# A two-layer attention and MLP kernel with its order written by a planner: four key passes, a second query block opened early, softmax sums by DMA, halved last blocks

## The chip, the cores and the metric

One core of a Trainium2 chip. The metric is the device time of one execution in microseconds; the shown time is the median of several runs. PE is the matrix engine (TensorE), ACT the scalar engine, DVE the vector engine, POOL GpSimd, SP the engine that issues most DMAs.

## The reference

Batch 1, 2048 rows, 448 columns, 16 heads of 28 columns, MLP width 1792, bf16 in and out.

```
x = x + attention(layernorm(x), wqkv, wo)       # 16 heads, softmax over all 2048 keys
x = x + mlp(layernorm(x))                       # relu(x w1 + b1)^2 w2 + b2
x = x + attention(layernorm(x), wqkv, wo)       # the same weights once more
x = x + mlp(layernorm(x))
```

Layer 0 is the first pair of lines, layer 1 the second.

## The kernel before

All weights, x, keys, queries and values stay in SBUF. Rows come in 16 tiles of 128; four tiles make a block of 512 queries. The 16 heads are four groups `g` of four heads, padded from 28 to 32 columns, so that four heads fill 128 partitions. The pad columns of `V_sb` hold 1.0, so that the values' matmul also sums the weights of the softmax: each head's row 28 of its 32 output rows is the sum.

Attention runs in units of one head, one tile of 128 keys and 512 queries. Three units make a group: three matmuls write scores into three PSUM banks (tile `sc`, L416, two such tiles), one exponential on ACT takes all three (128x1536, L431) and writes `pt` (four buffers), and three matmuls multiply by `V_sb` into the bank `oT` (L460, one bank). There are 683 groups, numbered here in the order of PE. A pass is a run of groups with one layer, query block and head group; it ends when DVE moves `oT` out. The first query block of a layer is made in two passes over the keys, with partial sums in `part_sb` (L475, L481): in layer 0 tiles 0 to 3 and then 4 to 15, in layer 1 tiles 0 to 11 and then 12 to 15. All other blocks take all keys in one pass.

Everything else goes through one PSUM bank, `ps_m`: transposes after a layer norm (`tp`, L312), K, Q and V tiles, the projection by `wo`, both MLP matmuls (all L335, in `mm_tile`), and `den` (L493), a matmul by `sel` that spreads each head's sum over its 32 rows, after which DVE takes a 128x512 reciprocal (L498) and multiplies (L505). Each such tile is one write by PE and one read by DVE, and the next tile waits for that read.

After the last pass of a query block, `norm_stream` normalises its four head groups, and `chain` does projection, layer norm, MLP, and in layer 0 the next layer's layer norm, keys, values and queries. Layer 1 needs keys from all four blocks of layer 0.

The order on each engine is written when the program is built, by `Planner`. Streams of operations have a priority (scores 0, exponentials 1, values 2, normalisation 3, chains 4 and up), each operation a duration, engines, dependencies and buffers from `Res` pools. Again and again the planner takes the operation that could start first; PE work that is not scores may not end more than 0.40 us after the next scores could start. On the chip each engine then keeps that order and waits on semaphores. An engine that waits holds back all that is queued behind it.

Of the kernel before, what the change touches and what calls it, by code (L numbers as in the profile page):

```python
# [13 lines left out]
P = 128  # L14
# [6 lines left out]
MAGIC = 0x5F3759DF  # L21


class Res:


    def __init__(self, n):
        self.free = [(0.0, i) for i in range(n)]


class Op:
    __slots__ = ("eng", "dur", "fn", "deps", "acq", "rel", "mode", "sets", "start", "end", "buf")

    def __init__(self, eng, dur, fn, deps=(), acq=None, rel=None, mode="full", sets=None):
        self.eng, self.dur, self.fn, self.deps = eng, dur, fn, deps
        self.acq, self.rel, self.mode, self.sets = acq, rel, mode, sets
        self.start = self.end = None


LAT = {"PE": 0.22, "ACT": 0.22, "DVE": 0.10, "POOL": 0.15, "DMA": 0.0}  # L40


class Planner:
# [13 lines left out]
    def earliest(self, o):  # L57
        t = 0.0
        for d in o.deps:
            if not isinstance(d, Op):  # L60
                d = self.tok.get(d)
            if d is None or d.end is None:
                return None, None
            lat = 0.06 if d.eng == o.eng == "DVE" else (0.0 if d.eng == o.eng else LAT[d.eng])
            t = max(t, d.end + lat)
        if o.acq is not None:
            if not o.acq.free:
                return None, None
            t = max(t, min(o.acq.free)[0])
        best = None  # L70
        for e in (o.eng if isinstance(o.eng, tuple) else (o.eng,)):
# [7 lines left out]
    def run(self):  # L79
        while self.streams:  # L80
# [6 lines left out]
            main = next((c for c in cands if c[1] == 0), None)  # L87
            if main is not None:
                cands = [
                    c for c in cands  # L90
                    if c[2] != "PE" or c[1] == 0 or c[0] + c[3][2].dur <= main[0] + 0.40
                ]
            s, _, e, st = min(cands, key=lambda c: (c[0], c[1]))
            o = st[2]
            o.eng = e
            if o.acq is not None:
                o.buf = min(o.acq.free)[1]
                o.acq.free.remove(min(o.acq.free))
# [5 lines left out]
            if o.rel is not None:  # L104
                res, of = o.rel if isinstance(o.rel, tuple) else (o.rel, None)
                res.free.append((o.end + LAT[e], of.buf if of else 0))
            if o.sets is not None:
                self.tok[o.sets] = o
# [6 lines left out]
def kernel(  # L115
# [16 lines left out]
    NQB = S // QB  # L132
    TPB = QB // P
# [3 lines left out]
    scale = float(DH) ** -0.5  # L137

# [6 lines left out]
    hp = ctx.enter_context(tc.tile_pool(name="hp", bufs=NFC + 1))  # L145
    rp = ctx.enter_context(tc.tile_pool(name="rp", bufs=2))
    np_ = ctx.enter_context(tc.tile_pool(name="np_", bufs=2))
    sp = ctx.enter_context(tc.tile_pool(name="sp", bufs=4))
    ps_sc = ctx.enter_context(tc.tile_pool(name="ps_sc", bufs=2, space=bass.MemoryType.PSUM))
# [6 lines left out]
    R_xt, R_os, R_xn = Res(3), Res(2), Res(2)  # L156
# [14 lines left out]
    Q_one = const.tile([P, G, S], DT.bfloat16, name="Q_sb")  # L171
    Q_sb = [Q_one, Q_one]
    V_sb = [const.tile([P, NTB, H, DHP], DT.bfloat16, name=f"V_sb{l}") for l in range(2)]
    part_sb = const.tile([P, G, QB], DT.float32, name="part_sb")
    part = [part_sb[:, g, :] for g in range(G)]
# [6 lines left out]
    def dma(out_ap, in_ap, nbytes, key):  # L182
        def fn(e):
            nc.sync.dma_start(out=out_ap, in_=in_ap)  # L184
        return Op("DMA", nbytes / 150e3, fn, sets=key)

    def setup():
        nc.vector.memset(warm[:], 0.0)
        nc.scalar.activation(out=warm[:], in_=warm[:], func=AF.Exp)
        nc.vector.memset(st_qk[DL:P, 3, :], 0.0)  # L190
        nc.vector.memset(wv[DL:P, 3, :], 0.0)
        nc.vector.memset(w1[DL:P, 3, :], 0.0)
        nc.gpsimd.memzero(wk[:])
        nc.gpsimd.memzero(wq[:])
        make_identity(nc, ident[:])
# [3 lines left out]
        nc.gpsimd.memset(V_sb[0][:], 1.0)  # L199
        nc.gpsimd.memset(sel[:], 0.0)  # L200
        nc.gpsimd.affine_select(
# [7 lines left out]
        )  # L209
        nc.gpsimd.memset(one0[:], 0.0)  # L210
        nc.gpsimd.memset(one0[0:1, :], 1.0)  # L211
        nc.gpsimd.memset(b2w[:], 0.0)  # L212
        nc.gpsimd.memzero(wo[:])  # L213
        nc.gpsimd.memset(V_sb[1][:], 1.0)  # L214

    def loads():
# [9 lines left out]
        for b in range(1, NQB):  # L226
            for hf in range(2):
                t0 = b * TPB + 2 * hf
                yield dma(x_sb[:, t0:t0 + 2, :], x_view[:, t0:t0 + 2, :], 224 * kb, ("x", b, hf))
        for hh in range(G):  # L230
# [8 lines left out]
    def wprep():  # L239
        def cp(dst, c0):  # L240
            def fn(e):
                src = st_qk[:, :, c0:c0 + D].rearrange("p c (h r) -> p c h r", r=DH)
                if e == "ACT":
                    nc.scalar.copy(out=dst[:, :, :, 0:DH], in_=src)
                else:
                    nc.vector.tensor_copy(out=dst[:, :, :, 0:DH], in_=src)
            return fn
        yield Op("ACT", 1.8, cp(wk, D), deps=[("wqk",)], sets=("wk",))
        yield Op("DVE", 1.0, cp(wq, 0), deps=[("wqk",)], sets=("wq",))

    def layernorm(blk, deps_of):


        mv = sp.tile([P, TPB, 2], DT.float32, name="mv")
        last = None
        for j in range(TPB):
            tb = blk * TPB + j

            def stats(e, tb=tb, j=j):
                st = sp.tile([P, 6], DT.float32, name="st")  # L260
                nc.vector.bn_stats(out=st[:, :], in_=x_sb[:, tb, :])  # L261
                nc.vector.bn_aggr(out=mv[:, j, :], in_=st[:, :])
            last = Op("DVE", 0.75, stats, deps=deps_of(j))
            yield last

        rstd = sp.tile([P, TPB], DT.float32, name="rstd")

# [342 lines left out]
```

## Time and profile before

| what | value |
|---|---|
| median of 3 runs | 1146.45 us (1145.83 to 1148.68) |
| the profiled execution | 1145.94 us, its span 1143.9 us |
| mean granted clock of PE | 0.876 |
| busy: PE, ACT, DVE | 950.2, 940.7, 500.9 us |
| exponentials (L431) | 683, 926.3 us |
| first exponential starts, last one ends | 29.26, 1074.0 us |

The span is the time from the first to the last instruction; the execution has some 2 us more around it. A group row of the page gives busy time and the mean of one, then the idle time ahead of it and what ended it. A timeline row gives start, length, engine, line, operation and what was idle before it. PE's busy time includes overlap within its pipeline, so a high share does not say that it is at its peak.

### The profile page before, as it was taken

What the parts mean: (1) busy time and instruction counts of PE and PEld (TensorE: products, weight loads), DVE (VectorE), ACT (ScalarE), POOL (GpSimd) and SP (SyncE); (2) the same over time, 40 slices, a digit from 0 to 9 for tenths busy, and PEclk for the clock granted to TensorE, in tenths of its full rate; (3) what the DMA queues carried; (4) which work ended last, traced back from release to release, by engine and by line L of the source; (5) the groups of instructions that cost most, each with busy time, mean ns of one, the idle gap of its engine ahead of it and who ended that gap; (6) DMA issues with size and microseconds to landing.
All of it is one profiled execution on the core that took longest, in us unless ns stands there. A gap on an engine that the chain in (4) does not pass through costs nothing.

```text
span 1143.9 us, 14096 instructions
## 1 busy us (share of the span) xinstructions
PE 950.2 (83%) x5804; PEld 312.1 (27%) x5856; DVE 500.9 (44%) x898; ACT 940.7 (82%) x705; POOL 22.7 (2%) x24
## 2 busy tenths in 40 slices
PE   2876878889898989899789967999889988899646
PEld 0222222323333323222223322222223222223112
DVE  8743313551556434553455245453245322551241
ACT  1763899999999999999579738899989999899511
POOL 6000000000000000000000000000000000000000
PEclk9998876899898998899889978699969986799569
DMA  7000000000000000000000000000000000000000
GB/s 233 1 1 1 1 1 1 1 1 1 1 1 1 1 1 1 2 1 1 1 1 1 1 1 1 1 1 5 13 1 1 5 13 1 1 1 17 0 1 16
DMA packets 7532, 9.38 MB, mean 8 GB/s; under 512 B 555, under 2 KB 6764, under 8 KB 7469
## 3 DMA queue, kind: packets, MB, share of 16 engines
q1 hardware_dynamic: 7084, 7.58, 2.1%
q8 instruction: 45, 0.74, 0.3%
q0 software_dynamic: 384, 0.92, 0.2%
q14 instruction: 19, 0.15, 0.0%
HBM read 6.66 MB, written 1.84 MB: 7 GB/s over the span
## 4 chain that ended last, share of the span: by engine, by line
issue 98%; POOL 1%; DMA 0%; SPq 0%; POOLq 0%
POOL V_sb L214 1%; DMA x_sb<-in_A_x_dram 0%; SPq L184 0%; POOL out_dram L558 0%; POOL wo L213 0%; POOLq L605 0%; POOL b2w L212 0%; POOL one L211 0%; POOLq L558 0%
## 5 line engine op out<-in xcount | busy, mean ns | idle before, releaser
L431 ACT ACTIVATE pt<-sc 128x1536 bf16<-128x1536 f32 (+1 forms) x683 | 926.3, 1538 | 112.9 <-PE sc L416 108.9
L416 PE MATMUL sc<-Q_sb,K_sb 32*128 32x512 bf16 x2048 | 298.3, 427 | 92.6 <-ACT pt L431 87.7
L460 PE MATMUL oT<-pt,V_sb 128*32 128x512 bf16 x2048 | 291.1, 429 | 7.1 <-DVE V_sb L373 3.9
L416 PEld LDWEIGHTS <-K_sb 32*128 32x128 bf16 x2048 | 86.9, 92 | 347.6 <-issue 340.4
L498 DVE RECIPROCAL rec<-den 128x512 f32<-128x512 f32 x32 | 107.4, 3355 | 64.9 <-PE den L493 64.9
L514 DVE TENSOR_TENSOR x_sb<-x_sb,mt 128x448 bf16<-128x448 bf16 x64 | 39.7, 620 | 216.3 <-PE mt L335 216.3
L335 PE MATMUL mt<-xnT,w 128*128 128x512 bf16 x417 | 119.5, 395 | 17.5 <-ACT r L534 9.1
L460 PEld LDWEIGHTS <-V_sb 128*32 128x32 bf16 x2048 | 68.1, 94 | 187.7 <-issue 176.4
L335 PE MATMUL mt<-w,h 128*128 128x448 bf16 x448 | 107.8, 356 | 3.7 <-DVE x_sb L514 2.3
L536 DVE TENSOR_SCALAR r<-mt 128x512 bf16<-128x512 f32 x98 | 67.8, 692 | 89.5 <-PE mt L335 89.5
L312 PE MATMUL tp<-ident,xn 128*128 128x128 bf16 x256 | 29.1, 282 | 40.6 <-DVE xn L300 37.2
L335 PEld LDWEIGHTS <-w 128*128 128x128 bf16 x448 | 39.7, 100 | 73.3 <-issue 43.6
L542 DVE TENSOR_TENSOR h<-r 128x512 bf16<-128x512 bf16 x112 | 47.5, 424 | 22.9 <-ACT r L534 19.9
L335 PE MATMUL mt<-wo,oTn 128*128 128x448 bf16 x128 | 39.7, 446 | 10.8 <-DVE x_sb L514 6.2
L335 PEld LDWEIGHTS <-h 128*128 128x128 bf16 x448 | 34.6, 97 | 51.5 <-issue 33.5
L534 ACT ACTIVATE r<-mt 128x512 bf16<-128x512 f32 x14 | 8.4, 597 | 43.1 <-PE mt L335 42.0
L493 PE MATMUL den<-oT_sb,sel 128*128 128x512 f32 x64 | 42.4, 750 | 0.9 <-DVE oT_sb L479 0.8
L335 PE MATMUL mt<-xnT,wk 128*128 128x512 bf16 x109 | 36.0, 420 | 8.6 <-DVE xnT L318 4.2
L335 PE MATMUL mt<-xnT,wq 128*128 128x512 bf16 x126 | 37.8, 425 | 6.3 <-DVE K_sb L350 3.9
L479 DVE COPY oT_sb<-oT 128x512 f32<-128x512 f32 x24 | 16.6, 690 | 55.8 <-PE oT L460 55.6
L350 DVE CAST Q_sb<-mt 128x512 bf16<-128x512 f32 x30 | 20.7, 692 | 41.2 <-PE mt L335 41.2
L261 DVE BATCH_NORM_STATS2 st<-x_sb 128x6 f32<-128x448 bf16 x64 | 38.6, 603 | 0.1
(53 smaller groups left out, 329.2 us busy)
## 6 DMA issues: line engine op xcount, KB each, us to landing
x_sb<-in_A_x_dram SPq DMA_DIRECT2D x8, 224.0 KB, 4.6
w<-in_B_w_dram SPq DMA_DIRECT2D x1, 1568.0 KB, 11.5
w<-in_B_w_dram SPq DMA_DIRECT2D x1, 1344.0 KB, 8.0
out_dram<-x_sb SPq DMA_DIRECT2D x8, 112.0 KB, 1.7
out_dram<-x_sb POOLq DMA_DIRECT2D x8, 112.0 KB, 1.9
part_sb<-in_A_wqkv_dram SPq DMA_DIRECT2D x1, 672.0 KB
wo<-in_A_wo_dram SPq DMA_DIRECT2D x4, 98.0 KB
wv<-in_A_wqkv_dram SPq DMA_DIRECT2D x1, 336.0 KB
```

The source lines that it names most:

```text
L261: nc.vector.bn_stats(out=st[:, :], in_=x_sb[:, tb, :])
L312: nc.tensor.transpose(out=tp[:, dc, k * P:(k + 1) * P], in_=xn[:, dc * P:(dc + 1) * P], identity=ident[:, :])
L335: nc.tensor.matmul(box["t"][:, 0:n], lhsT=lhsT, rhs=rhs, start=(i + k == 0), stop=(i + k == len(mms) - 1))
L350: nc.vector.tensor_copy(out=dst, in_=t[:, 0:QB])
L416: nc.tensor.matmul(sc[:, k * 512:(k + 1) * 512], lhsT=K_sb[l][r, g, kb * P:(kb + 1) * P], rhs=Q_sb[l][r, g, qb * QB:(qb + 1) * QB], start= ...
L431: nc.scalar.activation(out=pt[:, 0:n], in_=gbuf[gi]["sc"][:, 0:n], func=AF.Exp, scale=scale)
L460: nc.tensor.matmul(box["t"][DHP * hh:DHP * hh + DHP, :], lhsT=V_sb[l][:, kb, 4 * g + hh, :], rhs=gbuf[gi]["pt"][:, k * 512:(k + 1) * 512], ...
L493: nc.tensor.matmul(box["t"][:, :], lhsT=sel[:, :], rhs=res["t"][:, :], start=True, stop=True)
L498: nc.vector.reciprocal(out=rec[:, :], in_=box["t"][:, :])
L514: nc.vector.tensor_tensor(out=x_sb[:, tb, :], in0=x_sb[:, tb, :], in1=t[:, 0:D], op=ALU.add)
L536: nc.vector.tensor_scalar(out=r[:, :], in0=t[:, 0:QB], scalar1=0.0, scalar2=None, op0=ALU.max)
L542: nc.vector.tensor_tensor(out=h[:, :], in0=r[:, :], in1=r[:, :], op=ALU.mult)
```

## The change

1. Start: `V_sb` is filled with ones only in its pad columns, the second one and some constants later; the copies of `wk` and `wq` are cut in two and all run on ACT; block 0 may use `sc` banks beside `ps_m`, and ACT for its evacuations; 24 matmuls on zeros run first on PE.
2. Layer 0's first query block takes its keys in four passes of four tiles; key tiles are made ahead of values and queries for blocks 1 to 3.
3. In layer 1, query block 1 is begun (head groups 0 and 1, keys 0 to 11) before block 0 takes keys 12 to 15; its partial sums lie in the old `K_sb` of layer 0.
4. Normalisation, except in the last block of each layer: the four sum rows go by DMA from `oT_sb` to 128x16, DVE takes a small reciprocal, and two more DMAs bring it through DRAM back to 128x512 as `rec`.
5. The last query block of layer 1 is cut into two of 256 queries; a unit is then two key tiles, and MLP tiles hold two at a time in a bank.
6. When the last scores have been issued, the `sc` banks are lent to all tiles and ACT may evacuate.
7. The planner's latencies and durations differ, and PE work may end up to 0.7 us after the scores' inputs are ready. Stores of x all go by SP.

```diff
+WARM = 24
+AHEAD = range(2)
+SLACK = 0.7
-LAT = {"PE": 0.22, "ACT": 0.22, "DVE": 0.10, "POOL": 0.15, "DMA": 0.0}
+LAT = {"PE": 0.22, "ACT": 0.22, "DVE": 0.10, "POOL": 0.15, "DMA": 2.0}
...
-                    if c[2] != "PE" or c[1] == 0 or c[0] + c[3][2].dur <= main[0] + 0.40
+                ok = [c for c in cands if c[2] != "PE" or c[1] == 0 or c[0] + c[3][2].dur <= due + SLACK]
...
+    blocks = [[(0, 4), (4, 4), (8, 4), (12, 4)], [(0, 4), (4, 4), (8, 4), (12, 2), (14, 2)]]
...
-        nc.gpsimd.memset(V_sb[0][:], 1.0)
+        nc.gpsimd.memset(V_sb[0][:, :, :, DH:DHP], 1.0)
+        idle = ps_o.tile([P, QB], DT.float32, name="oT")
+        for _ in range(WARM):
+            nc.tensor.matmul(idle[:, 0:D], lhsT=b2w[:, 0:P], rhs=b2w[:, :], start=True, stop=True)
...
+    def pools_now(early=False):
+        return (R_m, R_sc) if early or len(s_left) == 0 else (R_m,)
+    def engs_now(early=False):
+        return ("ACT", "DVE") if early or len(s_left) == 0 else ("DVE",)
...
-        cut = 4 if l == 0 else NTB - 4
+    add_passes(0, [0], [0, 4, 8, 12, 16])
+    for qb in range(1, len(blocks[0])):
+        add_passes(0, [qb], [0, 16])
+    add_passes(1, [0], [0, 12])
+    add_passes(1, [1], [0, 12], AHEAD)
+    add_passes(1, [0], [12, 16])
+    add_passes(1, [1], [12, 16], AHEAD)
+    add_passes(1, [1], [0, 16], range(AHEAD[-1] + 1, G))
+    for qb in range(2, len(blocks[1])):
+        add_passes(1, [qb], [0, 16])
...
     def norm_stream(l, qb, g, res, oe):
+        tail = qb == len(blocks[l]) - 1
+        if tail:
...
+        else:
+            def spread(e):
+                box["d"] = sp.tile([P, QB // DHP], DT.float32, name="dn")
+                nc.sync.dma_start(out=box["d"][:, 0:w], in_=res["t"][DH::DHP, 0:n])
+            d1 = Op("DMA", 0.1, spread, deps=[oe])
+            def rcp(e):
+                nc.vector.reciprocal(out=box["d"][:, 0:w], in_=box["d"][:, 0:w])
+            r1 = Op("DVE", 0.25, rcp, deps=[d1])
+            def away(e):
+                box["s"] = dp.tile([P, w], DT.float32, name=f"scr{w}")
+                nc.sync.dma_start(out=box["s"][:, :], in_=box["d"][:, 0:w])
+            d2 = Op("DMA", 0.1, away, deps=[r1])
+            def back(e):
+                box["r"] = rp.tile([P, QB], DT.float32, name="rec")
+                src = box["s"][:, :].rearrange("(h a) j -> h (a j)", h=G)
+                nc.sync.dma_start(out=box["r"][:, 0:n], in_=src.unsqueeze(1).to_broadcast([G, DHP, n]))
+            r = own = Op("DMA", 1.0, back, deps=[d2], acq=R_rec)
```

What this does to the order, at three places. First DVE while the first query block runs, in before: it casts a key tile (`K_sb`) and a query tile by turns, and moves part sums (L475) between.

```order
L350 CAST K_sb_98<-mt 128x512
L475 COPY part_sb<-oT 128x512
L350 CAST Q_sb<-mt 128x512
L373 CAST V_sb_101<-mt 128x16x28 x4
L475 COPY part_sb<-oT 128x512
L350 CAST K_sb_98<-mt 128x512
L350 CAST Q_sb<-mt 128x512
L350 CAST K_sb_98<-mt 128x512
L350 CAST Q_sb<-mt 128x512
```

The same place in the changed kernel; L573 adds to the part sums.

```order
L401 CAST K_sb_100<-mt 128x512
L427 CAST V_sb_103<-mt 128x16x28
L573 TENSOR_TENSOR part_sb<-oT,part_sb 128x512
L427 CAST V_sb_103<-mt 128x16x28 x3
L573 TENSOR_TENSOR part_sb<-oT,part_sb 128x512
L401 CAST K_sb_100<-mt 128x512 x3
L573 TENSOR_TENSOR part_sb<-oT,part_sb 128x512
L401 CAST Q_sb<-mt 128x512 x4
```

A block's key tiles now stand together ahead of its query tiles, and passes end in between.

Second DVE where the first query block's sums are taken, in before, with `oT_sb` the finished output of one head group:

```order
L481 TENSOR_TENSOR oT_sb<-oT,part_sb 128x512
L350 CAST K_sb_98<-mt 128x512
L498 RECIPROCAL rec<-den 128x512
L505 TENSOR_TENSOR oTn<-oT_sb,rec 128x512
L350 CAST Q_sb<-mt 128x512
L350 CAST K_sb_98<-mt 128x512
```

And in the changed kernel, where `dn` is the 128x16 tile that a DMA has filled:

```order
L573 TENSOR_TENSOR oT_sb<-oT,part_sb 128x512
L401 CAST Q_sb<-mt 128x512
L610 RECIPROCAL dn<-dn 128x16
L401 CAST Q_sb<-mt 128x512 x2
L573 TENSOR_TENSOR oT_sb<-oT,part_sb 128x512
L633 TENSOR_TENSOR oTn<-oT_sb,rec 128x512
L401 CAST Q_sb<-mt 128x512
```

The large reciprocal is gone here, and its `den` on PE; the small one and the product are queued apart, with evacuations between and behind them, and three DMAs of SP lie between them.

Third ACT at the end of the program, in before:

```order
L348 CAST K_sb_98<-mt 128x512
L348 CAST Q_sb<-mt 128x512
L431 ACTIVATE pt<-sc 128x1536 x677
L431 ACTIVATE pt<-sc 128x1024
L534 ACTIVATE r<-mt 128x512 x14
```

And in the changed kernel:

```order
L517 ACTIVATE pt<-sc 128x1536 x677
L517 ACTIVATE pt<-sc 128x1024
L671 ACTIVATE r<-mt 128x512
L671 ACTIVATE r<-sc 128x512 x5
L358 COPY xnT<-sc 128x4x256
L671 ACTIVATE r<-mt 128x512
```

The MLP's first half after the last exponential now alternates between `ps_m` (`mt`) and the lent score banks (`sc`), and a transposed tile is copied out by ACT among them.

More of the change, by code (lines that the diff above doesn't have):

```diff
@@ L104, in run @@
             if o.rel is not None:
[L105 to L108, printed above, removed]
+                o.rel.res.rel[o.rel.turn] = o.end + LAT[e]
+            for key in o.sets:
+                self.tok[key] = o
             st[2] = next(st[1], None)
```

524 lines of the change are left out of this document (300 added, 224 removed).

## The prediction

> **What bounds the kernel now.** I read the page first (busy shares, slices, groups), then the exponentials alone by stretches, then the timeline where they thin out.
>
> ```profile
> PE 950.2 (83%) x5804; PEld 312.1 (27%) x5856; DVE 500.9 (44%) x898; ACT 940.7 (82%) x705; POOL 22.7 (2%) x24
> ACT  1763899999999999999579738899989999899511
> ...
> L431 ACT ACTIVATE pt<-sc 128x1536 bf16<-128x1536 f32 (+1 forms) x683 | 926.3, 1538 | 112.9 <-PE sc L416 108.9
> L498 DVE RECIPROCAL rec<-den 128x512 f32<-128x512 f32 x32 | 107.4, 3355 | 64.9 <-PE den L493 64.9
> L493 PE MATMUL den<-oT_sb,sel 128*128 128x512 f32 x64 | 42.4, 750 | 0.9 <-DVE oT_sb L479 0.8
> ```
>
> The 683 exponentials of L431 keep ACT busy for 926.3 us, 1.356 us each (the mean of 1538 ns counts overlap of neighbours twice), and the change keeps their number. The slices show ACT at nines in the middle and low at the start, around the change of layers and at the end; where L431 waits, it waits for PE's scores. So the span of 1143.9 us is 926.3 and 217.6 us in which no exponential runs. By stretch (length, then ACT busy in L431, then granted clock):
>
> ```profile
> 29.20:60.00 30.80, 23.27 (x18) 1.00 0.00 1
> 60.00:83.40 23.40, 12.11 (x9) 1.00 0.00 1
> 83.40:110.90 27.50, 8.16 (x6) 0.93 0.00 1
> 110.90:140.00 29.10, 26.03 (x19) 0.83 0.00 1
> 140.00:558.90 418.90, 407.65 (x302) 0.89 0.00 1
> 558.90:579.00 20.10, 0.00 (x0) 0.64 0.00 0
> 579.00:651.80 72.80, 72.00 (x53) 0.98 0.00 1
> 651.80:683.90 32.10, 7.18 (x6) 0.79 0.00 1
> 683.90:760.00 76.10, 66.43 (x49) 0.75 0.00 1
> 760.00:1074.10 314.10, 303.49 (x225) 0.87 0.02 5
> ```
>
> The time without exponentials: 29.2 us before the first; 7.5, 11.3, 19.3 and 3.1 (41.2 together) while the first query block waits for the keys of blocks 1 to 3; 11.3 in the body of layer 0; 20.1 at the change of layers; 0.8; then 24.9 and 9.7 where layer 1 waits for its last key block; 10.6 in the rest; 69.8 after the last. The start, the three places that wait for keys, and the tail make 195 of the 217.6. There PE is not full: it follows chains of tiles through the single bank `ps_m`. One such wait, in the timeline of ACT:
>
> ```profile
> 83.41 8.16 ACT L431 ACTIVATE pt<-sc 128x1536 bf16<-128x1536 f32 x6 [11.30 <-PE sc L416]
> ```
>
> **The change, part by part.**
>
> *Start.* From the timeline, and then the row of the first key tile:
>
> ```profile
> 6.58 3.54 DVE L271 TENSOR_SCALAR ve<-mv 128x4 f32<-128x4 f32 x1
> 7.95 1.68 ACT L244 COPY wk<-part_sb 128x1792 bf16<-128x1792 bf16 x1 [5.72 <-DMA part_sb<-in_A_wqkv_dram]
> ...
> 12.07 6.91 POOL L214 MEMSET V_sb<- 128x8192 bf16 x1
> 12.33 7.09 DVE L300 TENSOR_SCALAR xn<-x_sb,mv,rstd 128x448 bf16<-128x448 bf16 x2
> ```
>
> ```profile
> 20.86 0.39 DVE L300 TENSOR_SCALAR xn<-x_sb,mv,rstd 128x448 bf16<-128x448 bf16 x1
> ```
>
> ```profile
> 23.53 1.86 PE L335 MATMUL mt<-xnT,wk 128*128 128x512 bf16 x4 [0.78 <-DVE xnT L318]
> ```
>
> DVE stands still while POOL fills `V_sb`: 7.09 us for two normalisations, of which a later one takes 0.39, ending as POOL's fill ends; 3.54 us for a 4-column operation. The change fills only the pad columns (an eighth of the elements, about 1 us by 6.91/8; up to 6.9 if strides undo that) and puts the second fill behind the first keys. Then the small operations (2.2 us from 10.12 to 12.33 in these rows) end near 9, two normalisations near 9.8. Two statistics pairs and two fills now stand on DVE before the last normalisation, which ends near 13.5. With transposes 0.7 (a guess) and ACT's copy 1.0 (1.68 scaled from 1792 to 1024 elements): 15.3. A key and a query tile at 1.86 bring 19.2, three value tiles that now stand ahead of the scores 2.7 to 4.9 (1.02 warm, in the tail's rows, or 1.86, at 448 columns), scores 0.7. First exponential at 20.5 to 25; I take 22, the clock warming on the way. The 24 warming matmuls run on an empty PE and end before the transposes; I give them nothing.
>
> *Four passes.* In before the second pass wants keys 4 to 15 of group 0 at once, and tiles K1, Q1, K2, Q2 pile up between score groups. In the order of PE, priced by the rows below, the fill at score groups 21 to 40 needs 142% of ACT's time; in the changed order no twenty groups before the 600th need over 94%.
>
> ```profile
> 535.64 0.39 PE L416 MATMUL sc<-Q_sb,K_sb 32*128 32x512 bf16 x3
> 535.96 0.40 PE L460 MATMUL oT<-pt,V_sb 128*32 128x512 bf16 x3
> 536.29 0.74 PE L335 MATMUL mt<-w,h 128*128 128x448 bf16 x3
> 536.97 0.39 PE L416 MATMUL sc<-Q_sb,K_sb 32*128 32x512 bf16 x3
> ```
>
> By the starts: 0.32 for scores, 0.33 for values, 0.68 for three 448-column matmuls (0.19 each and 0.11 for the switch). The block passes need 49 tiles in some 76 groups, 2.1 us per tile; the bank's own cycle is 1.71 (1123.78 to 1125.49 below). That fits, tightly. Twelve more moves of part sums fall to DVE, 44% busy. I leave 6 us for the ramp and 6 for gaps: 12 of 41.2, bounds 6 and 20 (half).
>
> *Change of layers, layer 1 begun twice.* In before twelve MLP matmuls, four projection tiles, two transposes and a key tile stand between the 352nd and 353rd score group; that is the 20.1. Now four `den` tiles a block leave the bank (1.3 and 3.36 us each by the two groups on the page), and those key tiles stand some ten groups ahead of their use. 1 stays, the most likely late piece being that block's transposes. The last key block's key tiles stand at groups 425 to 435, and 32 inserted groups of query block 1 put their first use at 437: 2 for 24.9, 5 for 9.7. Bounds for all three: 2 and 40.
>
> *Sums by DMA.* 28 normalisations leave the bank; some 34 us of PE and 87 of DVE go, which bound nothing here. They gain three DMAs in a chain on SP, and DVE, in order, waits twice. The order is made for 2.1 us to land, and 3.0 for the broadcast back. The nearest row, 112 KB on the same queue, and the far one, a 224 KB load among others:
>
> ```profile
> x_sb<-in_A_x_dram SPq DMA_DIRECT2D x8, 224.0 KB, 4.6
> ...
> out_dram<-x_sb SPq DMA_DIRECT2D x8, 112.0 KB, 1.7
> ```
>
> At 1.7 DVE waits for nothing; at 4.6 it stands 2.5 and 4.1 us per normalisation, 185 in all. Behind it stand evacuations of the bank, behind them PE, and behind PE, with about 0.7 us in hand from two score banks, ACT. About half of the 56 waits have an evacuation next. I take 7 us, near the nearer row, bounds 0 and 60. The stores of x queued behind on SP have no one waiting.
>
> *Body and cold clock.* What stays in the filled stretches:
>
> ```profile
> 1065.08 0.61 PE L416 MATMUL sc<-Q_sb,K_sb 32*128 32x512 bf16 x3 [0.19 <-ACT pt L431]
> 1065.63 0.61 PE L460 MATMUL oT<-pt,V_sb 128*32 128x512 bf16 x3
> ```
>
> ```profile
> 1060.00:1070.00 10.00, 8.69 (x48) 2.25 (x45) 0.34 (x1) 10.00 (x9) 0.00 (x0) 0.50 0.00 0
> ```
>
> With scores and values alone (0.65 us of each 1.356) the granted clock falls to 0.50 and the pair takes some 1.15; a projection tile then (1.65, below) makes the group 1.4 late. The order still has about a dozen such lean stretches, so 12, 1 and 10.6 stay for 11.3, 0.8 and 10.6. The Trainium skill ("TensorE: Matmul & The Clock Gate", "Why this matters for your kernels") asks for no PE-idle gap over about 3 us, else the clock halves; by it these stretches, idle for 0.2 us at a time, would keep full clock. The rows disagree, and the sum goes by them.
>
> The halved blocks write 256 columns at a time with twice the weight loads. No row shows that: nothing extra if the three row strips still run side by side, 15 us if each piece takes 0.1 to 0.2 longer and PE overflows. I take 2.4, since PEld's busy 312 us lie under matmuls now.
>
> *Tail.*
>
> ```profile
> 1075.45 2.08 PE L493 MATMUL den<-oT_sb,sel 128*128 128x512 f32 x2 [0.78 <-DVE oT_sb L479]
> ```
>
> ```profile
> 1080.98 1.65 PE L335 MATMUL mt<-wo,oTn 128*128 128x448 bf16 x4 [3.45 <-DVE rec L498]
> ```
>
> ```profile
> 1096.19 1.03 PE L312 MATMUL tp<-ident,xn 128*128 128x128 bf16 x8 [6.47 <-DVE xn L300]
> ```
>
> ```profile
> 1123.78 1.02 PE L335 MATMUL mt<-xnT,w 128*128 128x512 bf16 x4 [0.90 <-ACT r L534]
> ```
>
> ```profile
> 1125.49 2.81 PE L335 MATMUL mt<-w,h 128*128 128x448 bf16 x14 [0.69 <-ACT r L534]
> ```
>
> ```profile
> 1140.57 0.54 POOL L558 DMA_DIRECT2D out_dram<-x_sb  x1 [6.88 <-DVE x_sb L514]
> ```
>
> Two tiles instead of four, three banks instead of one: sums 1, half a reciprocal 1.7, product and move 0.9, waits 0.9: 4.5. Two projections with adds 3.5. The normalisation made PE wait 6.47 for four tiles; two statistics fewer and one beside a projection leave 4. Transposes and copy 2. Seven packed tiles at 0.95 instead of fourteen at 1.71: 7. Two y tiles 6. Add, store, end 3.5 (1140.57 to 1143.9 is 3.3). That is 30.5. Six packed tiles and two y tiles of the other half-block are queued between, partly in gaps: 6.5 more. 37 for 69.8, bounds 32 and 46.
>
> **Sum.** 926.3 + 22 + 12 + 12 + 1 + 1 + 2 + 5 + 13 (10.6 and 2.4) + 37 + 7 = 1038.3. The profiled execution took 1145.94, 2.0 above its span; the median is 0.5 above that: 1041.
>
> **Rivals.**
> *The fill starves ACT (15%).* If a third of the body, 300 us, runs as 683.9 to 760 did, 13% without exponentials, that is 39 where I count 8: 1072. For it: fill at 90 to 94% of a clock that must be warm. Against: 579 to 651.8 lost 1%.
> *DMAs hold DVE (10%).* 1.4 us past the order's figure at the 28 waits with an evacuation behind: 39 over the 7: 1080. The Trainium skill ("DMA: Bandwidth & Descriptors", "Why a DMA increments its semaphore by 16 and not by 1") says that the number of engines must divide the outer size on both sides; spread and broadcast have a 4 on one side, so four of 16 would carry them. No run here shows it yet.
> *The clock stays full (9%).* Without the restarts 24 of the 27 us in the body go: 1017.
> *Chains still late (7%).* The change does not do what it says: the bank's chain is as long as before at the change of layers and the last keys, and 40 of 55 us come back: 1073 to 1081.
> *Slower (4%, of it 1% within 0.3%).* At the far DMA row, 185 us held and passed on to ACT whole, the time is 1219; it decides from 1.9 us per wait over all 56 (105 us). Against it stands the 1.7 us row.
>
> **How the numbers follow.** The likeliest case has 55%, with 1018 to 1066 from the terms' bounds. 1010 to 1085 takes in the clock case and most of the three late ones. Faster by over 0.3% (about what a measurement tells from no change) 95%, within 1%, slower 4%.
>
> **What would show it.** First exponential at 22; no wait of ACT over 3 us from there to the last; `dn` reciprocals and products that wait under 0.5 us for DMA; a tail under 40. Long waits of DVE for `dn` or `rec`, or ACT waiting 1 to 2 us throughout the filled stretches, make the forecast wrong.

## The result, and the profile after

The changed kernel takes 1012.34 us (median of four, 1005.88 to 1016.05) against 1146.28 for the kernel before in the same comparison: a ratio of 0.8822, 95% interval 0.8774 to 0.887. The forecast of 1041 named the right direction, and its range of 1010 to 1085 held the time by 2 us at the lower end; the time lies outside the 1018 to 1066 of its likeliest case: the change brought 134 us where 105 were forecast. The profiled execution took 1013.62, its span is 1011.8. One of the six executions of the kernel without lending (1049.97 us) was in the chip's slower state and is left out of its median and ratio below.

The page of the changed kernel, the parts that answer to those of before (busy shares, slices, exponentials, products):

```profile
PE 907.4 (90%) x6400; PEld 311.0 (31%) x6400; DVE 416.8 (41%) x929; ACT 943.9 (93%) x712; POOL 5.1 (1%) x14
ACT  4999998899999999999999999998899999999982
PEclk7999967899989989899798998767997996679989
...
L517 ACT ACTIVATE pt<-sc 128x1536 bf16<-128x1536 f32 (+1 forms) x683 | 924.6, 1517 | 30.3 <-PE sc L502 28.6
L633 DVE TENSOR_TENSOR oTn<-oT_sb,rec 128x512 bf16<-128x512 f32 (+1 forms) x36 | 22.7, 631 | 63.4 <-DMA rec<-scr 63.2
```

The exponentials are as many and as long as before. Their wait for PE's scores fell from 108.9 to 28.6 us, and the three valleys in ACT's slices are gone. New is the wait of DVE for the broadcast `rec`, 63.2 us. By stretch (length, ACT busy in the exponentials, granted clock of PE):

```profile
24.09:153.77 129.68, 127.93 (x95) 0.93 0.05 16
153.77:515.00 361.23, 343.94 (x254) 0.92 0.02 7
515.00:560.00 45.00, 44.51 (x34) 0.92 0.00 1
560.00:670.00 110.00, 109.85 (x82) 0.86 0.03 8
670.00:980.40 310.40, 298.33 (x221) 0.86 0.05 15
```

The differences of the first two numbers are the time without exponentials: 1.8 us in the region of the four passes, 17.3 in the body of layer 0, 0.5 at the change of layers, 0.2 at the last key block, 12.1 in the rest. With 24.1 ahead of the first exponential and 31.4 behind the last (980.4 to 1011.8) these are the 87 us beside the 924.6.

What is left in the two bodies has two forms. The first, on the timelines of DVE, PE and ACT around 188 us:

```profile
186.52 0.69 DVE L633 TENSOR_TENSOR oTn<-oT_sb,rec 128x512 bf16<-128x512 f32 x1 [4.23 <-DMA rec<-scr]
187.13 0.68 DVE L673 TENSOR_SCALAR r<-mt 128x512 bf16<-128x512 f32 x1
...
187.87 1.01 PE L385 MATMUL mt<-xnT,w 128*128 128x512 bf16 x2 [3.58 <-DVE r L673]
...
189.53 1.45 ACT L517 ACTIVATE pt<-sc 128x1536 bf16<-128x1536 f32 x1 [3.60 <-PE sc L502]
```

DVE stands 4.23 us for the broadcast; the evacuation `r` behind it is late; PE, in order, stands 3.58; ACT 3.60. It is the chain of the prediction, link by link. The second form is the restart after a stretch of scores and values alone, DVE, PE and ACT around 155 us:

```profile
153.48 0.69 DVE L633 TENSOR_TENSOR oTn<-oT_sb,rec 128x512 bf16<-128x512 f32 x1 [6.38 <-DMA rec<-scr]
...
152.22 1.30 PE L385 MATMUL mt<-wo,oTn 128*128 128x448 bf16 x3
154.23 0.56 PE L385 MATMUL mt<-wo,oTn 128*128 128x448 bf16 x1 [0.71 <-DVE oTn L633]
154.72 0.61 PE L502 MATMUL sc<-Q_sb,K_sb 32*128 32x512 bf16 x3
...
155.43 1.45 ACT L517 ACTIVATE pt<-sc 128x1536 bf16<-128x1536 f32 x1 [1.67 <-PE sc L502]
```

Three matmuls of a projection take 1.30 us here and 0.74 in the prediction's row of a warm stretch, and the next scores come 1.67 us late. Not all of that is the slow PE: 0.71 of it is PE's wait for the product `oTn`, which had itself stood 6.38 us for `rec`. The two forms meet at this place.

### The profile page after: what moved, and what is told of

It is laid out like the page before. It is cut to its first block, busy times and chain, and to the rows that moved or that the text cites. A ratio compares the mean times of both kernels' runs of the same rounds, so it can differ in the third digit from the quotient of the medians.

```text
span 1011.8 us, 15410 instructions
## 1 busy us (share of the span) xinstructions
PE 907.4 (90%) x6400; PEld 311.0 (31%) x6400; DVE 416.8 (41%) x929; ACT 943.9 (93%) x712; POOL 5.1 (1%) x14
## 4 chain that ended last, share of the span: by engine, by line
ACT 45%; PE 21%; issue 17%; DMA 10%; DVE 6%; SPq 0%; ACTq 0%; DVEq 0%
ACT pt L517 45%; PE mt L385 8%; DMA rec<-scr 6%; PE sc L502 5%; PE oT L548 4%; PE sc L385 2%; DMA scr<-dn 2%; PE tp L350 2%; DMA dn<-oT_sb 1%; DVE r L673 1%; DVE rec L595 1%; DVE oTn L633 1%; DMA x_sb<-in_A_x_dram 1%; DVE K_sb L401 1%; DVE x_sb L644 0%
## 5 line engine op out<-in xcount | busy, mean ns | idle before, releaser
L517 ACT ACTIVATE pt<-sc 128x1536 bf16<-128x1536 f32 (+1 forms) x683 | 924.6, 1517 | 30.3 <-PE sc L502 28.6
L502 PE MATMUL sc<-Q_sb,K_sb 32*128 32x512 bf16 (+1 forms) x2304 | 294.1, 394 | 61.2 <-ACT pt L517 59.8
L548 PE MATMUL oT<-pt,V_sb 128*32 128x512 bf16 (+1 forms) x2304 | 296.1, 400 | 6.0 <-ACT pt L517 3.0
L385 PE MATMUL mt<-xnT,w 128*128 128x512 bf16 (+1 forms) x432 | 117.1, 390 | 13.2 <-DVE r L673 7.6
L385 PE MATMUL mt<-w,h 128*128 128x448 bf16 x406 | 93.7, 356 | 1.3 <-DVE rec L595 0.5
L633 DVE TENSOR_TENSOR oTn<-oT_sb,rec 128x512 bf16<-128x512 f32 (+1 forms) x36 | 22.7, 631 | 63.4 <-DMA rec<-scr 63.2
L401 DVE CAST K_sb<-mt 128x512 bf16<-128x512 f32 x30 | 20.7, 690 | 38.7 <-PE mt L385 38.7
L385 PE MATMUL mt<-wo,oTn 128*128 128x448 bf16 x124 | 33.3, 384 | 3.7 <-DVE oTn L633 2.5
L360 DVE COPY xnT<-tp 128x1024 bf16<-128x1024 bf16 x29 | 20.1, 692 | 37.7 <-PE tp L350 37.5
L401 DVE CAST Q_sb<-mt 128x512 bf16<-128x512 f32 x30 | 20.7, 691 | 34.3 <-PE mt L385 34.3
L427 DVE CAST V_sb<-mt 128x448 bf16<-128x448 f32 x29 | 18.1, 625 | 35.7 <-PE mt L385 35.7
L385 PE MATMUL mt<-wv,xnT 128*128 128x448 bf16 x120 | 28.2, 353 | 1.4
```

The source lines that it names most:

```text
L360: nc.vector.tensor_copy(out=dst, in_=tp[:, :, 0:w])
L385: nc.tensor.matmul(box["t"][:, c0:c0 + n], lhsT=lhsT, rhs=rhs, start=a, stop=b)
L401: nc.vector.tensor_copy(out=dst, in_=src)
L502: nc.tensor.matmul(sc[:, c0:c0 + nt * P], lhsT=K_sb[l][rows, g, (kb + i) * P:(kb + i + 1) * P], rhs=Q_sb[rows, g, t0 * P:(t0 + nt) * P], s ...
L517: nc.scalar.activation(out=pt[:, 0:n], in_=gbuf[gi]["sc"][:, 0:n], func=AF.Exp, scale=scale)
L548: nc.tensor.matmul(box["t"][DHP * hh:DHP * hh + DHP, 0:n], lhsT=V_sb[l][:, kb + i, 4 * g + hh, :], rhs=gbuf[gi]["pt"][:, c0:c0 + n], start ...
```

## The experiments

Theory: the time comes from PE's order at the places where ACT waited, each part of the change has its own place, and what stays are DVE's waits for DMA and the cold restarts. The rivals: one part did it all (the bank that the sums left), and the rest is a matter of the clock alone. Each kernel is the changed one with one edit; "more" and "less" are against its median, 1012.34 for the first four edits and 1011.88 for the others. The kernel before took 1144.3 to 1146.3 us in these comparisons and the changed kernel's own executions spread by 1%, so a few microseconds of difference say little. Not undone one by one are the planner's durations, latencies and slack (part 7), the key tiles made ahead in layer 0, and the copies and extra banks of the start.

| edit | median, us (runs) | ratio to before, 95% | gaps of ACT, first to last exponential | behind the last exponential |
|---|---|---|---|---|
| none | 1012.34 (4) | 0.8822 (0.8774 to 0.887) | 29.0 | 31.4 |
| none, again | 1011.88 (5) | 0.8828 (0.8807 to 0.8848) | 31.1 | 31.4 |
| layer 1 opens one block | 1039.83 (4) | 0.9088 (0.9066 to 0.9109) | 55.6 | 30.2 |
| sums by matmul | 1033.80 (4) | 0.9036 (0.9017 to 0.9055) | 39.5 | 42.9 |
| layer 0 in two passes | 1042.87 (4) | 0.9115 (0.9094 to 0.9135) | 60.6 | 30.4 |
| last block whole | 1029.58 (4) | 0.9005 (0.8975 to 0.9035) | 26.9 | 50.5 |
| no lending | 1043.12 (5) | 0.9103 (0.9064 to 0.9143) | 26.2 | 60.1 |
| broadcast as four DMAs | 1001.08 (6) | 0.8740 (0.8714 to 0.8766) | 17.9 | 30.6 |
| lean scores computed twice | 1002.00 (6) | 0.8752 (0.8719 to 0.8786) | 15.1 | 30.2 |
| order made for the slow DMA | 1002.89 (6) | 0.8757 (0.8733 to 0.8780) | 14.9 | 31.6 |
| four DMAs and scores twice | 995.20 (4) | 0.8690 (0.8664 to 0.8715) | 9.4 | 30.3 |
| no warming matmuls | 1004.31 (1) | | 22.2 | 30.6 |
| full fill of V | 1012.35 (1) | | 27.4 | 30.5 |

The last two columns are from the profiled executions. The gaps are ACT's waits of over 0.15 us; with the shorter ones and three evacuations by ACT, the 29.0 of the first row are the some 32 us without exponentials of the section before. Where an edit does not touch the body (the two without edit, the whole block, no lending, the last two rows), the gaps are 22 to 31, 27 in the mean: that is their own spread.

**One block opened early.**

```diff
-    add_passes(1, [0], [0, 12])
-    add_passes(1, [1], [0, 12], AHEAD)
-    add_passes(1, [0], [12, 16])
-    add_passes(1, [1], [12, 16], AHEAD)
-    add_passes(1, [1], [0, 16], range(AHEAD[-1] + 1, G))
+    add_passes(1, [0], [0, 12, 16])
+    add_passes(1, [1], [0, 16])
```

> Layer 1 opens only its first query block early: keys 0 to 11 and then 12 to 15 of all four groups, and no group of block 1 between them; everything else as in the changed kernel (1012 us, ratio 0.882). Theory A, the order gives the time: the 32 inserted score groups are what lets the last key block's tiles come in time, so most of the 24.9 and 9.7 us of before come back, 20 to 35 us, 1032 to 1047. Theory B, the bank gives the time: the bank, rid of the den tiles, is quick enough alone, and the key tiles arrive in time or nearly so, 0 to 8 us, 1012 to 1020. The place shows it: ACT waiting for scores at the first key group of the last block, about 10 to 25 us at a time under A, under 5 under B.

The time rose by 27.5 us. ACT's timeline where the last key block is first used:

```profile
612.97 4.13 ACT L514 ACTIVATE pt<-sc 128x1536 bf16<-128x1536 f32 x3 [20.33 <-PE sc L499]
625.12 20.31 ACT L514 ACTIVATE pt<-sc 128x1536 bf16<-128x1536 f32 x15 [4.58 <-PE sc L499]
647.13 14.88 ACT L514 ACTIVATE pt<-sc 128x1536 bf16<-128x1536 f32 x11 [1.70 <-PE sc L499]
```

The waits are back at that place, so the 32 inserted groups are what covers the last key tiles. Over the same groups, 592.6 to 699.7 us here and 651.8 to 760.0 in before, no exponential runs for 31.7 us here and for 34.6 there: all else that changed, the freed bank included, took 3 of the 34.6.

**Sums by matmul.**

```diff
-        tail = qb == len(blocks[l]) - 1
+        tail = True
```

> All 36 softmax sums by matmul and a reciprocal of the whole tile again, no DMA; all else as changed. Theory A, the bank's time is what counts: 28 den tiles of 1.3 us on PE and some 4.7 us each of the bank come back, 36 us of PE into an engine that is 90% busy and 130 us of the bank's time: 20 to 60 us more, 1032 to 1072, with waits of ACT of 5 to 20 us at the change of layers. Rival, the new DMA waits cost as much as they save: DVE stood 78 us behind DMA, so without them the time is the same or up to 10 us lower, 1002 to 1012.

21.5 us more, the low end of the first theory, and both theories hold in part. One long wait came back, at the change of layers, as long as in the kernel before (20.1):

```profile
531.41 4.14 ACT L517 ACTIVATE pt<-sc 128x1536 bf16<-128x1536 f32 x3 [20.42 <-PE sc L502]
```

On PE's timeline its chain is seen; the bank goes from hand to hand:

```profile
510.05 1.13 PE L589 MATMUL den<-oT_sb,sel 128*128 128x512 f32 x2
...
514.77 0.73 PE L385 MATMUL mt<-wo,oTn 128*128 128x448 bf16 x3 [3.27 <-DVE rec L595]
...
519.72 1.65 PE L385 MATMUL mt<-wo,oTn 128*128 128x448 bf16 x4 [3.30 <-DVE x_sb L644]
```

At the last key block no long wait came back: the longest behind this one is 1.4 us. The tail is 11.5 longer because the first half-block is late: its projection runs at 991.5 us, behind the last exponential (989.4), where in the changed kernel its MLP tiles run at 977.7, ahead of the last exponential (980.4). Without the 20.4, the gaps of the body are 19 us; in the six rows of the table that leave the body alone they are 27 in the mean (22 to 31). So the DMA sums gain at two places, and the bodies are some 8 us (3 to 12) worse with them. Those 8 us are not the price of DVE's waits alone, since the clock changed too. The stretch ahead of 155 us, here with the sums on PE (length, PE, weight loads, DVE, ACT, POOL, granted clock, DMA share, GB/s):

```profile
130.00:150.00 20.00, 15.81 (x108) 5.10 (x105) 13.40 (x10) 20.00 (x16) 0.00 (x0) 1.00 0.01 2
```

In the changed kernel the clock of these 20 us is 0.62 (its row stands below, at the scores that are computed twice), and the mean of the execution is 0.924 here and 0.895 there.

**Layer 0 in two passes.**

```diff
-    add_passes(0, [0], [0, 4, 8, 12, 16])
+    add_passes(0, [0], [0, 4, 16])
```

> Layer 0 takes its keys in two passes (0 to 3, 4 to 15) as before; all else as changed, with the short fill of V and the DMA sums. Theory A: the stalls are PE's order, 142% of ACT's time in 20 score groups, and come back whole: 25 to 35 us more, 1037 to 1047, in two or three waits of ACT of 7 to 19 us between 30 and 130 us. Rival: part of the 41.2 us was the late V fill and a clock or DVE disturbance, and only 8 to 15 us return, 1020 to 1027.

30.5 us more:

```profile
71.97 4.13 ACT L517 ACTIVATE pt<-sc 128x1536 bf16<-128x1536 f32 x3 [12.43 <-PE sc L502]
101.17 4.13 ACT L517 ACTIVATE pt<-sc 128x1536 bf16<-128x1536 f32 x3 [19.44 <-PE sc L502]
```

12.4 and 19.4 us, next to 11.3 and 19.3 before: these two come with the order of the passes. Of the 7.5 and 3.1 us that before lost ahead of and behind them, 1.7 and 1.4 stand here.

**Last block whole.**

```diff
-... [(0, 4), (4, 4), (8, 4), (12, 2), (14, 2)]]
+... [(0, 4), (4, 4), (8, 4), (12, 4)]]
```

> The last query block of layer 1 stays whole (four tiles of 128 queries); idle score banks still lent. Theory A, halving and lending each give half of the tail's gain: the tail grows from 31 to 45 us by 0.9 for the sum, 1.6 for the reciprocal, 2 for two projections, 2.5 for the normalisation, 1.5 for transposes, 6 for seven more tiles at 0.87, 5.6 for two more y tiles, less some 7 to 10 for the other half-block that is queued there now: 1022 to 1027. Rival B, lending alone does nearly all: under 5 us more. Rival C, the halved blocks cost body time (twice the weight loads): the body gives back as much as the tail loses, no change.

17.2 us more: 50.5 behind the last exponential for 31.4. The body did not shorten beyond its spread (26.9), so the halved blocks cost it nothing that can be seen. PE in this tail, up to the transposes:

```profile
985.75 1.12 PE L385 MATMUL sc<-wo,oTn 128*128 128x448 bf16 x5 [3.06 <-DVE oTn L633]
986.71 1.65 PE L385 MATMUL mt<-wo,oTn 128*128 128x448 bf16 x4
988.15 1.70 PE L385 MATMUL sc<-wo,oTn 128*128 128x448 bf16 x4
996.32 1.03 PE L350 MATMUL sc<-ident,xn 128*128 128x128 bf16 x8 [6.47 <-DVE xn L338]
```

A whole block has nothing to do on PE during the 6.47 us of its normalisation. With halves, the other half's tiles stand there, and PE waited 1.59 in the changed kernel:

```profile
993.21 0.70 PE L350 MATMUL sc<-ident,xn 128*128 128x128 bf16 x8 [1.59 <-DVE xn L338]
```

**No lending.**

```diff
-        return (R_m, R_sc) if early or len(s_left) == 0 else (R_m,)
+        return (R_m, R_sc) if early else (R_m,)
-        return ("ACT", "DVE") if early or len(s_left) == 0 else ("DVE",)
+        return ("ACT", "DVE") if early else ("DVE",)
```

> After the last score group no score bank and no ACT for the other tiles (lending taken out; the start keeps its own); halved blocks stay. Theory: in the tail each packed tile then takes 1.7 us through the one bank with DVE's move instead of 0.87, 13 tiles of both half-blocks in all, 11 us, and the transposes' and projections' moves 2 more: tail 40 to 46 instead of 31, 1021 to 1027. Rival: the chain of sum, reciprocal, statistics sets the tail and the tiles fit beside it: under 4 us more.

31 us more, at least twice what was expected. The same kind of tile on PE, first without lending, then in the changed kernel:

```profile
984.51 1.03 PE L385 MATMUL mt<-xnT,w 128*128 128x256 bf16 x8 [0.78 <-DVE r L673]
...
1004.91 1.03 PE L350 MATMUL tp<-ident,xn 128*128 128x128 bf16 x8 [5.00 <-DVE xn L338]
...
1009.38 1.86 PE L385 MATMUL mt<-xnT,w 128*128 128x256 bf16 x8 [0.78 <-DVE r L673]
1012.03 1.86 PE L385 MATMUL mt<-xnT,w 128*128 128x256 bf16 x8 [0.78 <-DVE r L673]
```

```profile
996.58 1.04 PE L385 MATMUL mt<-xnT,w 128*128 128x256 bf16 x8
997.46 1.91 PE L385 MATMUL sc<-xnT,w 128*128 128x256 bf16 x16
999.20 1.04 PE L385 MATMUL mt<-xnT,w 128*128 128x256 bf16 x8
```

Through one bank PE waits 0.78 us for DVE at each tile. At 984.51 the clock is still full, and a tile takes 1.82 from start to start, near the expected 1.7. Then PE stands 5.00 us for the normalisation, the granted clock falls to 0.50, and the tiles behind it take 2.65, their eight matmuls 1.86 instead of 1.03. The expectation had no slow clock in it. With lending the tiles follow each other at 0.87 and a full clock; the stretches are without and with lending:

```profile
1010.00:1015.00 5.00, 3.44 (x16) 2.10 (x15) 2.16 (x4) 0.00 (x0) 0.00 (x0) 0.50 0.00 0
```

```profile
1000.00:1005.00 5.00, 5.00 (x40) 3.62 (x38) 2.13 (x5) 2.39 (x4) 0.00 (x0) 1.00 0.01 3
```

These rows hold the length of the stretch, PE, weight loads, DVE, ACT, POOL, then the clock.

**The broadcast as four DMAs.**

```diff
-                nc.sync.dma_start(out=box["r"][:, 0:n], in_=src.unsqueeze(1).to_broadcast([G, DHP, n]))
+                for h in range(G):
+                    nc.sync.dma_start(out=box["r"][DHP * h:DHP * h + DHP, 0:n],
+                                      in_=src[h:h + 1, :].to_broadcast([DHP, n]))
```

> The broadcast of the reciprocals goes back as four DMAs, one for each head, 32 partitions of one row each, instead of one DMA over (4, 32, 512). Theory, the outer size sets how many engines carry it (Trainium skill, DMA: Bandwidth & Descriptors, Why a DMA increments its semaphore by 16 and not by 1): the landing falls from 4.7 to 5.3 us to about 3, DVE's wait for rec from 63 to under 25 us, and the waits of 3.6 and 2.55 us of ACT at 189 and 727 us go: 4 to 8 us less, 1004 to 1008. Rival, the time is issue and latency and four issues on one queue take longer: landing 5 to 7 us, the wait 80 us or more, 0 to 10 us more.

10.8 us less, more than expected, though DVE's wait for `rec` fell from 60.6 to 28.8 us and not under 25. ACT's wait for scores fell from 30.7 to 17.5; the waits at 189 and 727 us, 3.60 and 2.55 in the changed kernel, are 1.96 and 0.68. One microsecond of the single broadcast, then one of the four (the last two numbers are the mean busy share of the 16 DMA engines and GB/s):

```profile
398.00:399.00 1.00, 0.65 (x9) 0.28 (x6) 0.17 (x1) 1.00 (x2) 0.00 (x0) 1.00 0.26 100
```

```profile
389.00:390.00 1.00, 0.38 (x9) 0.17 (x6) 0.00 (x0) 1.00 (x2) 0.00 (x0) 1.00 0.59 131
```

A busy share of 0.26 is about what four engines of 16 at full load would give. This is what the Trainium skill ("DMA: Bandwidth & Descriptors", "Why a DMA increments its semaphore by 16 and not by 1") gives for an outer size of 4; the trace agrees. The four small ones reach 0.59, but the rate only rises from 100 to 131 GB/s. The whole gain is not a quick landing, however: one issue became four, here in SP's queue and in the chain that ended last:

```profile
385.95 2.93 SPq L624 DMA_DIRECT2D rec<-scr  x4
```

```profile
388.46 2.08 DMA rec<-scr
```

The last part lands at 390.54, 4.6 us after its source was there; mostly the four issues take 1.7 us and it is 3.3 to 3.8. The single one, of 256 KB, took 4.7 to 5.5. So up to about 1.7 us are saved each time; that this is enough fits an order made for 3.0, but was not traced wait by wait.

**Scores of lean stretches twice.**

```diff
+                lean = lean + 1 if pl.fill == seen else 0
+                seen = pl.fill
-                for i in range(4):
+                for i in [*range(4)] * (2 if lean >= 2 else 1):
```

`pl.fill` counts PE's operations that are neither scores nor values.

> Where two score groups in a row have nothing but values between them on PE, the scores from the second on are computed twice into the same bank (some 110 of 683 groups, 0.3 us each, in PE's idle time); nothing else is changed. Theory, cold restarts: PE in these lean stretches is idle half the time and the granted clock falls to 0.5; with it warm, the waits of ACT right after them (2.9 at 155, 1.8 at 309, 1.8 at 700, 1.8 at 894 and smaller ones, some 15 to 18 us together) go: 8 to 16 us less, 996 to 1004. Rival, the clock is lost all over and not through idle PE (a budget of work): the granted clock in the lean stretches stays under 0.7 or falls elsewhere, and the time is the same or up to 10 us more.

9.9 us less, and ACT's wait for scores 14.7 us. The stretch ahead of the restart at 155 us, in the changed kernel and here:

```profile
130.00:150.00 20.00, 15.99 (x93) 4.46 (x90) 4.55 (x9) 20.00 (x16) 0.00 (x0) 0.62 0.10 30
```

```profile
130.00:150.00 20.00, 13.81 (x132) 4.42 (x130) 4.54 (x9) 20.00 (x16) 0.00 (x0) 0.99 0.10 30
```

With 39 matmuls more in the same 20 us PE is busy for less time, at a clock of 0.99 instead of 0.62. DVE's wait for `rec` hardly changed (57.3), so half of what ACT lost goes without a quicker DMA. The waits named at 309, 700 and 894 us shrank from 1.16, 1.46 and 1.46 to 0.85 and twice under 0.5; at 155 us 1.37 of 1.67 stayed, with PE still standing 0.67 for the late product there. The budget theory falls: the mean clock of the execution rose from 0.887 to 0.950.

**The order made for the slow DMA.**

```diff
-            r = own = Op("DMA", 1.0, back, deps=[d2], acq=R_rec)
+            r = own = Op("DMA", 3.6, back, deps=[d2], acq=R_rec)
```

> One DMA for the broadcast as in the changed kernel, but the order is made for 5.6 us to its landing instead of 3.0. Theory, DVE is held because the order puts the product 2 us too early, and what stands behind it is late: the wait of DVE for rec falls from 61 to under 25 us and the time by 4 to 10 us, 1002 to 1008, without a quicker transfer. Rival, what counts is the quick transfer itself (the projection tiles stand too late for PE, which has nothing to do): DVE's wait falls but the lean stretches grow by 2.6 us each, and the time stays at 1009 to 1016.

9.0 us less with the same slow transfer, so the order that is made around it counts, not the speed alone. But the wait of DVE is still 47.9 us, in 11 places instead of 23: the expected fall under 25 did not come. What changed is which work stands behind those waits; that was not traced place by place.

**Both together.**

> Both at once: the scores of lean stretches computed twice, and the broadcast as four DMAs. Alone they gave 9.9 and 10.8 us (1002.0 and 1001.1 for 1011.9). If one takes away what the cold clock costs and the other what DVE's waits cost, the two sums add, 989 to 995, with waits of ACT for scores under 10 us in all. If both only relieve the same places (the tiles right behind a lean stretch, where oTn is also late), they don't add: 997 to 1002.

995.20 us: the version that beats both kernels, 1.6% under the changed one and 13.1% under the kernel before. 16.7 us of the 20.7 that the two gave alone: they share some places. In the gaps of the table, the four DMAs take 9 us from the mean of 27 at the low clock (17.9) and 5.7 at the high one (15.1 to 9.4); the doubled scores take 12 and 8.5. The exponentials of this version:

```profile
L523 ACT ACTIVATE pt<-sc 128x1536 bf16<-128x1536 f32 (+1 forms) x683 | 925.2, 1524 | 11.5 <-PE sc L508 9.0
```

**The start.** `WARM = 0` instead of 24; and `V_sb[0]` filled whole instead of in its pad columns.

> The 24 matmuls on an empty PE at the start are left out. Theory: they give nothing, since the first key tile still takes 1.86 us: first exponential at 24 us, within 0.5. Rival: they shorten the time to the full clock, and the value tiles at 20 to 23 us come out cold without them: first exponential 1 to 3 us later.

> POOL fills the whole of layer 0's V at the start again, 8192 columns instead of 1024 of them; all else as changed. Theory: DVE stands still while POOL fills, the last normalisation ends 4 to 6 us later and the first exponential runs at 28 to 30 us instead of 24.1. Rival: the start is bounded by the load of the weights and by PE, and the first exponential moves by under 1 us.

Without the warming matmuls the first exponential ran at 22.9 us (one execution, 1004.31 us in all, next to the 1005.88 of the changed kernel's quickest); in the kernels that leave the start alone it ran at 22.3 to 24.1. They give nothing that can be seen: the first key tile takes 1.86 us with them and 1.87 without, and the first eight matmuls of the value tiles take 2.67 with them and 2.15 without, so the rival falls too.

```profile
16.83 1.86 PE L385 MATMUL sc<-xnT,wk 128*128 128x512 bf16 x4 [1.10 <-ACT xnT L358]
```

```profile
16.18 1.87 PE L385 MATMUL sc<-xnT,wk 128*128 128x512 bf16 x4 [1.10 <-ACT xnT L358]
```

The granted clock tells more. The 24 matmuls end at 7.83 us; between there and the key tile PE waits 1.71, 2.46, 1.81 and 1.10 us for normalisations and their copies, and the granted clock, 0.99 from 8 to 12 us, is 0.50 from 12 to 22 (the columns are as above):

```profile
12.00:22.00 10.00, 6.39 (x21) 2.67 (x22) 9.01 (x31) 3.91 (x6) 0.00 (x0) 0.50 0.74 228
```

With the full fill of layer 0's values the first exponential ran at 25.6 (one execution), 1.5 to 3.3 later: between the two theories. POOL fills from 3.02 to 9.94, and a DVE operation of four columns, 0.17 us in the changed kernel, does not end until 10.11:

```profile
3.02 6.92 POOL L214 MEMSET V_sb<- 128x8192 bf16 x1
```

```profile
6.61 3.50 DVE L309 TENSOR_SCALAR ve<-mv 128x4 f32<-128x4 f32 x1
```

The first normalisations end 3.2 us later, and the wait for x and some slack take back a part. DVE does not stand still for the whole fill, as the prediction says: the four statistics ahead of that operation run beside it, from 3.55 to 6.4 us, at 0.59 to 0.63 us each as without it. The kernel before fills twice, layer 0's values at the same time as here and layer 1's from 12.07 to 18.98:

```profile
3.03 6.92 POOL L199 MEMSET V_sb<- 128x8192 bf16 x1
```

This run puts back the first fill alone. The second, beside which two normalisations took 7.09 us in before, was not put back, so what it is worth stays open. In the changed kernel each fill of pad columns takes 0.95 us, as estimated; the second runs from 4.86 us, not behind the first keys.

## Why the prediction came out as it did

The forecast span was 1038.3, the measured one 1011.8. Term by term:

| term | forecast | measured | difference |
|---|---|---|---|
| 683 exponentials | 926.3 | 924.6 | -1.7 |
| start | 22 | 24.1 | +2.1 |
| four-pass region | 12 | 1.8 | -10.2 |
| change of layers, 0.8, last keys | 9 (1+1+2+5) | 0.7 | -8.3 |
| bodies, with DMA holds and halved blocks | 32 (12+13+7) | 29.4 | -2.6 |
| tail | 37 | 31.4 | -5.6 |

*What held.* ACT's chain of exponentials is the bound, the time lost is lost at named places, and the parts of the change close their own places: three of the undoing experiments put back the waits at that place to within a few microseconds of the kernel before.

*What was luck.* The range held by its margin, not by its terms. Three terms came out under their own lower bounds (1.8 for 6, 0.7 for 2, 31.4 for 32), and with every term at its lower bound and nothing for the halves the sum gives 1013, above the measured 1012. The terms' bounds do not give the 1018 to 1066 of the likeliest case either. What reached down to 1010 was the room for a clock that stays full, and the clock did not (mean 0.895).

*The step that failed* is the allowance at the places that were to close. For the four passes I took the tile cycle (1.71 us of 2.1) for "tight" and left a third of the stall; for the last keys I left 7. Next to nothing was left (1.8 and 0.7): at these places, where the order puts the tile ahead of its use and PE's load stays under ACT's time, the wait did not shrink, it went. The test was in the prediction (no twenty groups over 94%), and I allowed against it.

*The start* was 2.1 longer. The working ahead of it adds up to 22.6 to 24.8, and I took 22, with the clock warming on the way; the key and query tiles ran at 0.50. The last normalisation also ended at 15.1 and not at 13.5.

*The bodies* were right in sum, and the two causes were named. The DMA holds: 7 us forecast with bounds 0 and 60; the sums by matmul show some 8, the clock's part included, and the quicker broadcast takes 6 to 9 away. DVE waited 77.8 us (63.2 for `rec`, 14.6 for `dn`), not the 0 of the near row, nor the 185 of the far one: the broadcast took 4.7 to 5.5 us like the 4.6 row, the two small transfers mostly 1.4 to 1.9 like the 1.7 row. By the prediction's own signs this part of the mechanism was wrong: it expected reciprocals and products that wait under 0.5 us, and it called long waits of DVE a mark of a wrong forecast; single waits reached 6.6 us, and one wait of ACT (3.60) passed the 3 us that it allowed. That ACT lost so little of the 77.8 fits the other half of the term, that a wait costs only where an evacuation stands next. The cold restarts: two of the three kernels that shorten the bodies do it without touching the clock in the stretch ahead of 155 us (0.61 with the four DMAs, 0.56 with the other order), and doubling the scores does it without touching the DMA; each takes 9 to 12 us from the gaps' mean of 27. With both together 17.6 of the 27 go, so some 3 to 4 us count for both: a late `oTn` right behind a cold stretch is one wait with two causes.

*Halved blocks*: 2.4 forecast, nothing measured. Six matmuls of 256 columns take as long as three of 512, in the last block of the changed kernel:

```profile
970.38 0.40 PE L502 MATMUL sc<-Q_sb,K_sb 32*128 32x256 bf16 x6 [0.62 <-ACT pt L517]
970.71 0.40 PE L548 MATMUL oT<-pt,V_sb 128*32 128x256 bf16 x6
```

0.33 us from the one to the other, as before.

*The tail* came out 5.6 shorter, a little under the lower bound of 32: the other half-block's tiles fitted into the gaps almost whole (the 6.5 added for them was the mis-sized part), and the packed tiles took 0.87, not 0.95. By the starts on PE the steps of the last half-block (to the projection, to the transposes, to the packed tiles, to the y tiles, to the end) took 5.0, 7.8, 3.4, 6.1 and 9.1 us, where the forecast had 4.5, 7.5, 2, 7 and 9.5 before the 6.5. Undone alone, halving is worth 19.1 us of the tail and lending 28.7; that is what each adds to the other, and not a split.

*The rivals.* Fill that starves ACT, chains still late, slower: none was seen. Of the DMA rival the mechanism was there (four of 16 engines), with DVE's wait at 78 us, and the price was not, under 10 us instead of 46. Of the clock rival the other way round: the clock did not stay full, yet made to stay fuller (0.950) it gives 10 us, not 24.

## What to carry to other kernels

Where one engine sets the pace and the others follow an order written in advance, price the fill per place against that engine's time: at the three places undone here a stall of 20 to 32 us appeared where the order asked too much at once, and next to nothing remained where it did not, so an allowance in between was no estimate. A DMA in a chain belongs in the order with its measured landing (9.0 us here), and a broadcast over a size of 4 is worth cutting in pieces (10.8 us here). Work on an idle PE pays right up to the burst that needs the clock: doubled scores in the stretches ahead of bursts gave 10 us, warming matmuls followed by waits of 1 to 2.5 us gave none.

## What was not expected of the hardware

- The granted clock falls to 0.5 not only behind a long wait of PE, but in a steady stretch of scores and values. In the changed kernel PE's waits from 130 to 135 us are 0.47 to 0.62 us in each 1.35 at a full clock; from 135 to 150 us the granted clock is 0.50, and the same work mostly leaves waits of 0.18. The Trainium skill ("TensorE: Matmul & The Clock Gate", "Why this matters for your kernels") speaks of idle gaps over about 3 us; here gaps under 1 us were enough.
- In the tail without lending it is the other way: tiles with a wait of 0.78 us in every 1.82 ran at a full clock at 984 us, the clock fell with a wait of 5.00 us, and tiles with a wait of 0.78 in every 2.65 then ran at 0.50.
- The 24 matmuls from 1.19 to 7.83 us left no trace in the key tile at 16.83: by 12 us the clock was back at 0.50.
- The changed kernel's first four executions spread by 1% (1005.88 to 1016.05) and five later ones by 0.7%; the kernel before spread by 0.25% in its first four and by 0.4 to 0.7% in later sets. The quickest of the first four had the highest mean clock (0.901) and the slowest the lowest (0.890).
